# Two transformer layers on one core: norm arithmetic moved to GpSimd, reciprocals spread by DMA, and the two ends of the schedule reordered

## The chip, the core and the metric

The kernel runs on one core of one Trainium2 chip. A core has five engines that run side by side: TensorE (PE, the matmuls; PEld are its weight loads), VectorE (DVE), ScalarE (ACT), GpSimd (POOL) and SyncE (SP, which here issues DMAs). They share an on-chip memory of 128 partitions; matmuls write to a second one, PSUM, of eight banks per partition, here 512 fp32 columns each. The metric is the device time of one execution in microseconds, the median of several runs. Lower is better.

## The reference

Two layers of attention and feed-forward on 2048 rows of 512 features, both layers with the same weights. Attention has 32 heads of only 16 features each; the feed-forward part has 1792 hidden features.

```python
def _layernorm(x, axis=-1, eps=1e-5):
    m = jnp.mean(x, axis=axis, keepdims=True)
    v = jnp.var(x, axis=axis, keepdims=True)
    return (x - m) / jnp.sqrt(v + eps)

def _A_ref(x, wqkv, wo):                     # S = 2048, D = 512, H = 32, Dh = 16
    q, k, v = ...                            # x @ wqkv, split into 32 heads
    scores = jnp.einsum("bhqd,bhkd->bhqk", q, k) * (Dh ** -0.5)
    p = _softmax(scores, axis=-1)
    o = jnp.einsum("bhqk,bhkd->bhqd", p, v)
    return o.reshape(B, S, D) @ wo           # (after a transpose of heads and rows)

def _B_ref(x, w1, w2):                       # w1: 512 x 1792, w2: 1792 x 512
    return jnp.maximum(x @ w1, 0) @ w2

x = A_x
x = x + _A_ref(_layernorm(x), A_wqkv, A_wo)
x = x + _B_ref(_layernorm(x), B_w1, B_w2)
x = x + _A_ref(_layernorm(x), A_wqkv, A_wo)
x = x + _B_ref(_layernorm(x), B_w1, B_w2)
```

Per layer there are 32 heads x 2048 x 2048 scores, and each needs an exponential.

## The kernel before

The kernel is a Python program that writes the instruction stream of each engine. While it does so it keeps estimates of where PE and VectorE stand (`now_pe`, `now_dve`) and decides with them what comes next. The estimates are of use only for the order: the order is fixed when the kernel is built.

**The unit of work.** A score block is 128 keys x 512 queries of one head (256 queries in the last part of layer two). A *segment* is one chunk of queries and one set of heads; it has up to 64 blocks (16 key blocks x 4 heads that run side by side in PE). In each *slot* PE writes the scores of three blocks into three PSUM banks, and ScalarE takes the exponential of all three in one instruction. In some slots VectorE takes the third block instead: it builds the exponential by integer arithmetic on the bits. Two such blocks make a *pair*, and a pair goes through a chain of steps.

```python
ex = nc.scalar.activation(                   # L1323: 3 blocks, or 2 when VectorE takes one
    out=eb[:, 0 : place[m]], in_=b[:, 0 : place[m]], func=ACTF.Exp,
    scale=1.0 / (LOG2E * UNIT),
)
...
first = nc.vector.tensor_scalar(             # L1008: VectorE's block, out of PSUM
    out=lin[which][:, half * QS : (half + 1) * QS], in0=src, scalar1=EXP_BIAS,
    scalar2=0.0, op0=ALU.add, op1=ALU.max,
)
...
steps = (                                    # chain(): the rest, on both blocks at once
    (342, lambda: bits(0x7F, 0x3F80)),                                           # step
    (609, lambda: nc.vector.tensor_mul(out=power, in0=mantissa, in1=mantissa)),  # cube
    (342, lambda: ...),                      # scaling by a constant, mostly left out
    (342, lambda: bits(0x7F80, 0)),                                              # step
    (609, lambda: nc.vector.tensor_mul(                                          # cube
        out=power.bitcast(BF16), in0=power, in1=line.bitcast(BF16))),
)
```

A pair is begun when the schedule's conditions allow it: among others at most five pairs may be open, in the first layer the last value block must have been made (one pair may be open before), and the estimate of VectorE's queue must be short enough.

```python
elif (not pairs or pair_no[0] + 1 - pairs[0]["n"] < NP) and (
    (mine['l'] or ("v", 0, 15) in made or not pairs and ("k", 0, 0, 1) in made) and ...):
    queued = sum(t["cost"] for t in dve_q if "chain" in t)
    ...
    if now_dve[0] + waiting < now_pe[0] + BACKLOG:
        ...
```

**Order on VectorE.** VectorE's tasks wait in a queue and are taken by rank; the steps of a pair come last, unless their segment is the current one and nearly over.

```python
def rank(t):
    if "chain" not in t:
        return 2
    sg = t["chain"]["sg"]
    return 1.5 if sg is segs[seg_at[0]] and sg["left"] <= HASTE else 3     # HASTE = 12
...
for sg, kb, g in taken:          # taken: only the blocks that go to VectorE
    sg["left"] -= 1
```

**The value matmuls.** The blocks are multiplied with the values and summed over keys into one PSUM bank, `ps_o` (L914). Right after its exponentials a slot makes sure that the values of its key blocks exist:

```python
for sg, kb, g in now:
    run_until(("v", sg["l"], kb))
```

**End of a segment.** An extra column of ones in the values gives the sums for the softmax. Where a segment covers only some of the keys, its sums are stored and added later (`sg["load"]`). At the end the sums are copied to `u`, a small DMA brings the row of sums into a packed form `c`, VectorE takes reciprocals, and another DMA brings them back into `u`. Then they must be spread over the 32 partitions of each head: either by a GpSimd-issued DMA, or, where it must be quick, by a VectorE shuffle.

```python
quick = sg["load"] is not None or ended[l, j] == NT
def recip():
    nc.vector.reciprocal(out=c, in_=c)
    nc.sync.dma_start(out=sums, in_=c)
    if not quick:
        nc.gpsimd.dma_start(out=r[:, 0:width], in_=...)    # L863, sums spread to 32 partitions
    ...
def spread():
    nc.vector.stream_shuffle(out=r[:, 0:width], in_=u[:, 0:width], mask=[lane] * 32)   # L873
def spread_mul():
    if quick:
        spread()
    mul(0, width)                                                                      # L849
```

**The norm.** For each chunk of rows VectorE makes statistics and aggregates them, then the inverse root is taken: a seed from the bits of the number, and three Newton steps, in the middle of the run on GpSimd (`ln_newton`), in the first and the last norm on VectorE.

```python
def ln_stats(tag, tt, i):
    nc.vector.bn_stats(out=st[:], in_=x_t[tt][:])
    nc.vector.bn_aggr(out=mv[ln_n(tag)][:, i, :], in_=st[:])

def ln_rstd(tag, part):
    if part == 0:
        nc.vector.tensor_scalar(out=a[:], in0=mv[n][:, :, 1], scalar1=EPS, ...)         # L485
        nc.vector.tensor_scalar(out=t1[:], ..., op0=ALU.logical_shift_right)            # L488
        nc.vector.tensor_scalar(out=y[:], ..., scalar2=float(RSQRT_SEED), ...)          # L492
        return
    ...                          # one Newton step, 3 operations on VectorE

def ln_newton(tag):
    for _ in range(3):           # 4 operations each, on GpSimd
        ...
```

**The start.** Warming matmuls, the first norm, a transpose of its rows by PE with copies alternating between VectorE and ScalarE, then the first keys, queries and two value groups, and only then the loop of slots.

**The end.** After the last slot: the last segment's sums, the output projection, the last norm, and the feed-forward part of the last 256 rows, with its weights `w1buf` loaded four ahead.

Of the kernel before, what the change touches and what calls it, by code (L numbers as in the profile page):

```python
# [19 lines left out]
EPS = 1e-5  # L20
RSQRT_SEED = 0x5F3759DF
# [3 lines left out]
def kernel(  # L25
# [55 lines left out]
    RSTD_LAG = 5000.0  # L81
# [22 lines left out]
    masks = sb([P, 4], FP32, "masks")  # L104
# [51 lines left out]
    stats = [sb([P, nc.vector.BN_STATS_DIM], FP32, f"stats{n}") for n in range(2)]  # L156
# [23 lines left out]
    nc.gpsimd.memset(warm[:], 0.0)  # L180
    nc.vector.memset(ebuf[0][:, 0:QS], 0.0)
# [166 lines left out]
    def rank(t):  # L348
        if "chain" not in t:
            return 2  # L350
        sg = t["chain"]["sg"]
        return 1.5 if sg is segs[seg_at[0]] and sg["left"] <= HASTE else 3
# [120 lines left out]
    def ln_stats(tag, tt, i):  # L473
        if tag not in ln_seq:
            ln_seq.append(tag)
        st = stats[i % 2]
        nc.vector.bn_stats(out=st[:], in_=x_t[tt][:])  # L477
        nc.vector.bn_aggr(out=mv[ln_n(tag)][:, i, :], in_=st[:])

    def ln_rstd(tag, part):  # L480

        n = ln_n(tag)
        a, y, t1 = va_[n], ya_[n], ta_[n]
        if part == 0:
            nc.vector.tensor_scalar(  # L485
                out=a[:], in0=mv[n][:, :, 1], scalar1=EPS, scalar2=None, op0=ALU.add
            )
            nc.vector.tensor_scalar(  # L488
                out=t1[:].bitcast(I32), in0=a[:].bitcast(I32), scalar1=1, scalar2=None,
                op0=ALU.logical_shift_right,  # L490
            )
            nc.vector.tensor_scalar(  # L492
                out=y[:].bitcast(I32), in0=t1[:].bitcast(I32), scalar1=-1.0,
                scalar2=float(RSQRT_SEED), op0=ALU.mult, op1=ALU.add,
            )
            return
        nc.vector.scalar_tensor_tensor(
            out=t1[:], in0=y[:], scalar=-0.5, in1=y[:], op0=ALU.mult, op1=ALU.mult
        )
        nc.vector.tensor_mul(out=t1[:], in0=t1[:], in1=a[:])  # L500
        nc.vector.scalar_tensor_tensor(
            out=y[:], in0=t1[:], scalar=1.5, in1=y[:], op0=ALU.add, op1=ALU.mult
        )

    def ln_newton(tag):

        n = ln_n(tag)
        a, y, t1 = va_[n], ya_[n], ta_[n]
        for _ in range(3):
            nc.gpsimd.tensor_mul(out=t1, in0=y, in1=y)  # L510
            nc.gpsimd.tensor_mul(out=t1, in0=t1, in1=a)
            nc.gpsimd.tensor_scalar(
# [968 lines left out]
```

## Time and profile before

| | before |
|---|---|
| device time, median of 3 runs | 1611.67 us (1610.54 to 1612.03) |
| profiled execution, span | 1606.2 us |
| ScalarE busy | 1558.0 us (97%) |
| VectorE busy | 1505.7 us (94%) |
| PE busy (pipelined, modelled ends) | 1446.1 us (90%) |
| GpSimd busy | 92.9 us (6%) |
| exponentials on ScalarE (L1323) | 1366 instructions |
| blocks on VectorE (L1008) | 680, in 340 pairs |
| norm statistics / aggregations on VectorE | 64 / 64 |
| shuffles of reciprocals on VectorE (L873) | 28 |
| broadcasts of reciprocals by DMA (L863) | 52 |

How to read the lines of a profile: L1323 is line 1323 of the kernel; then come the engine and the operation, output<-input with partitions x elements and type, and the count. After the first bar stand busy time in us and the mean of one in ns, after the second the idle time of that engine just ahead of these instructions and what ended it ("<-PE ps_s L1314": a matmul into `ps_s`). A line of the time line begins with start and length in us. A busy share is an average over the run; a wait counts only on the engine that sets the end.

### The profile page before, as it was taken

To read this page: it belongs to the slowest core of one execution; us is meant where nothing else is said; L and a number is where in the kernel's file an instruction comes from. 1 tells how busy PE (TensorE), PEld (TensorE's weight loads), DVE (VectorE), ACT (ScalarE), POOL (GpSimd) and SP (SyncE) were. 2 spreads that over 40 slices of the span, in tenths; PEclk is the share of its full clock that TensorE was granted. 3 is DMA by queue.
4 is the path that set the end of the run, shared out by engine and by line. 5 is a ranking of instruction groups with operands and counts; after the bars stand their busy time and mean duration, and the time that the engine had idled before them with its cause. 6 is when DMAs were issued, how large, how long until landed. Compare 5 with 4: busy or idle time off the path is not lost. (4 is left out here: it accounts for less than half of the span.)

```text
span 1606.2 us, 45384 instructions
## 1 busy us (share of the span) xinstructions
PE 1446.1 (90%) x19833; PEld 541.9 (34%) x19833; DVE 1505.7 (94%) x3012; ACT 1558.0 (97%) x1385; POOL 92.9 (6%) x279
## 2 busy tenths in 40 slices
PE   7988888999999988999889998889989999998997
PEld 3322222322332332232223333223334444544454
DVE  7779999999999999999899999899999999999994
ACT  6999999999999999999999999999999999999994
POOL 2000001000010010100100000001001010010100
PEclk9999999999999999999999999999999999999999
DMA  5000000210001100120001000000210211212031
GB/s 164 2 2 2 2 2 9 47 29 10 9 17 40 28 16 2 27 50 10 15 2 27 21 2 1 2 4 9 54 24 17 42 30 29 59 28 54 14 62 47
DMA packets 113928, 40.61 MB, mean 25 GB/s; under 512 B 103328, under 2 KB 111264, under 8 KB 113728
## 3 DMA queue, kind: packets, MB, share of 16 engines
q1 hardware_dynamic: 101696, 26.21, 7.2%
q0 software_dynamic: 10688, 10.18, 3.6%
q8 instruction: 155, 2.54, 0.7%
q10 hardware_dynamic: 1344, 1.31, 0.2%
q14 instruction: 45, 0.37, 0.1%
HBM read 24.38 MB, written 2.10 MB: 16 GB/s over the span
## 5 line engine op out<-in xcount | busy, mean ns | idle before, releaser
L1323 ACT ACTIVATE e<-ps_s 128x1536 bf16<-128x1536 f32 (+1 forms) x1366 | 1548.1, 1364 | 12.4 <-PE ps_s L1314 7.7
L1314 PE MATMUL ps_s<-q,ktp 32*128 32x512 bf16 (+1 forms) x6192 | 613.6, 341 | 112.2 <-ACT e L1323 97.5
L914 PE MATMUL ps_o<-e,vaug 128*32 128x512 bf16 (+1 forms) x4262 | 501.0, 346 | 16.6 <-DVE u L836 6.8
L1008 DVE TENSOR_SCALAR lin<-ps_s 128x512 int16<-128x512 f32 x680 | 462.3, 684 | 32.9 <-PE ps_s L1314 27.4
L1314 PEld LDWEIGHTS <-ktp 32*128 32x128 bf16 x6192 | 199.9, 91 | 561.5 <-issue 417.5
L914 PEld LDWEIGHTS <-vaug 128*32 128x32 bf16 x6032 | 171.5, 94 | 305.0 <-issue 286.2
L1049 DVE TENSOR_SCALAR step<-lin 128x1024 int16<-128x1024 int16 x680 | 266.2, 417 | 1.1 <-PE ps_o L914 0.4
L1060 DVE TENSOR_TENSOR cube<-step 128x1024 f16<-128x1024 bf16 x340 | 230.2, 680 | 0.9
L1064 DVE TENSOR_TENSOR cube<-cube,lin 128x1024 bf16<-128x1024 f16 x340 | 229.5, 677 | 0.0
L914 PE MATMUL ps_o<-step,vaug 128*32 128x512 bf16 (+1 forms) x858 | 154.3, 341 | 0.0
L442 PE MATMUL ps_f<-xnT,w 128*32 128x512 bf16 (+1 forms) x2016 | 147.4, 345 | 5.7 <-DVE ht L695 3.7
L442 PE MATMUL ps_f<-w,ht 128*32 128x512 bf16 x1624 | 147.1, 381 | 1.6 <-DVE q L637 0.6
L914 PE MATMUL ps_o<-cube,vthird 128*32 128x512 bf16 (+1 forms) x804 | 140.0, 339 | 0.0
L914 PE MATMUL ps_o<-lin,vaug 128*32 128x512 bf16 (+1 forms) x858 | 118.9, 341 | 4.6 <-DVE u L836 3.7
L442 PE MATMUL ps_f<-xnT,wqkv 128*32 128x512 bf16 (+1 forms) x1312 | 106.7, 363 | 3.6 <-DVE vaug L623 1.8
L863 POOL DMA_DIRECT2D r<-u x52 | 36.9, 710 | 1170.2 <-DVE step L1049 383.3
L442 PE MATMUL ps_f<-wo,ot 128*32 128x512 bf16 x960 | 87.1, 381 | 1.5 <-DVE x L661 0.7
L695 DVE TENSOR_SCALAR ht<-ps_f 128x512 bf16<-128x512 f32 x105 | 71.8, 684 | 3.6 <-PE ps_f L442 3.0
L442 PEld LDWEIGHTS <-w 128*32 128x32 bf16 x2016 | 58.4, 96 | 36.0 <-issue 19.2
L637 DVE TENSOR_TENSOR q<-ps_f,masks 128x1024 bf16<-128x1024 f32 (+1 forms) x51 | 53.5, 1049 | 3.5 <-PE ps_s L1314 2.6
L442 PEld LDWEIGHTS <-ht 128*32 128x32 bf16 x1624 | 47.0, 96 | 27.3 <-issue 12.1
L849 DVE SCALAR_TENSOR_TENSOR ot<-u,masks,r 128x512 bf16<-128x512 f32 (+2 forms) x82 | 51.0, 624 | 1.1
(86 smaller groups left out, 653.4 us busy)
## 6 DMA issues: line engine op xcount, KB each, us to landing
w<-in_B_w_dram SPq DMA_DIRECT2D x140, 128.0 KB
r<-u POOLq DMA_DIRECT2D x25, 256.0 KB, 7.3
r<-u POOLq DMA_DIRECT2D x27, 128.0 KB, 4.9
out_dram<-x SPq DMA_DIRECT2D x16, 128.0 KB
x<-in_A_x_dram SPq DMA_DIRECT2D x14, 128.0 KB
w<-in_B_w_dram SPq DMA_DIRECT2D x1, 1792.0 KB
wqkv<-in_A_wqkv_dram ACTq DMA_DIRECT2D x2, 512.0 KB
c<-u SPq DMA_DIRECT2D x48, 8.0 KB
```

The lines of the kernel that those rows point to most:

```text
L442: nc.tensor.matmul(out[cols], lhsT[:, cols], rhs, start=i % k == 0, stop=i % k == k - 1, tile_position=(0, 32 * g), skip_group_check=True,)
L637: return nc.vector.tensor_mul(out=qbuf[n % 2][:, :, 0:w], in0=b.rearrange("p (e q) -> p e q", e=1).to_broadcast((P, 2, w)), in1=qmask.rear ...
L695: nc.vector.tensor_scalar(out=out, in0=sums, scalar1=0.0, scalar2=None, op0=ALU.max)
L849: nc.vector.scalar_tensor_tensor(out=ot[t][:, at_column + a : at_column + a + w], in0=u[:, a : a + w], scalar=mask[e], in1=r[:, a : a + w] ...
L863: nc.gpsimd.dma_start(out=r[:, 0:width], in_=bass.AP(tensor=sums.tensor, offset=sums.offset, ap=[list(sums.ap[0]), [0, 32], [1, width]],),)
L914: nc.tensor.matmul(ps_o[32 * g : 32 * g + 32, 0 : sg["w"]], values[:, 4 * sg["T"] + g, 2 * e : 2 * e + 32], rhs, start=g not in sg["begun" ...
L1008: first = nc.vector.tensor_scalar(out=lin[which][:, half * QS : (half + 1) * QS], in0=src, scalar1=EXP_BIAS, scalar2=0.0, op0=ALU.add, op1 ...
L1049: nc.vector.tensor_scalar(out=stair, in0=line, scalar1=keep, scalar2=put, op0=ALU.bitwise_and, op1=ALU.bitwise_or,)
L1060: (609, lambda: nc.vector.tensor_mul(out=power, in0=mantissa, in1=mantissa)),
L1064: (609, lambda: nc.vector.tensor_mul(out=power.bitcast(BF16), in0=power, in1=line.bitcast(BF16))),
L1314: nc.tensor.matmul(b[:, a : a + sg["w"]], kt[32 * g : 32 * g + 32, kc : kc + P], qbuf[sg["n"] % 2][32 * g : 32 * g + 32, sg["e"], 0 : sg[" ...
L1323: ex = nc.scalar.activation(out=eb[:, 0 : place[m]], in_=b[:, 0 : place[m]], func=ACTF.Exp, scale=1.0 / (LOG2E * UNIT),)
```

## The change

The norm in the middle of the run leaves VectorE but for its statistics: nine small GpSimd operations aggregate, add epsilon and take the inverse root with a power. The first and the last norm stay on VectorE with a seed in one operation and two refining steps instead of three. Stored sums that are longer than four key blocks (those of the first layer's first chunk) get their reciprocals spread by DMA, and where the shuffle is kept, it and the multiply are two tasks. Values are made when the value matmuls want them and no longer at each slot. The counter `left` counts every block, and the haste rule holds for any segment. At the start the copies, the first value groups and the order of keys and queries change; at the end the last sums are used right out of PSUM, and the last chunk's weights are loaded a stage ahead into buffers that are free by then.

```diff
+    nc.gpsimd.memset(masks[:, 4:5], -0.5)
-    RSTD_LAG = 5000.0
+    RSTD_LAG = 4000.0
@@ rank
-        return 1.5 if sg is segs[seg_at[0]] and sg["left"] <= HASTE else 3
+        return 1.5 if sg["left"] <= HASTE else 3
@@ norm, middle of the run
-        nc.vector.bn_stats(out=st[:], in_=x_t[tt][:])
-        nc.vector.bn_aggr(out=mv[ln_n(tag)][:, i, :], in_=st[:])
+        nc.vector.bn_stats(out=stats[ln_n(tag)][:, i, :], in_=x_t[tt][:])
+            pool = nc.gpsimd
+            pool.tensor_tensor(out=t1, in0=st[:, :, 1], in1=st[:, :, 4], op=ALU.subtract)
+            pool.tensor_mul(out=t1, in0=t1, in1=t1)
+            pool.tensor_scalar(out=t1, in0=t1, scalar1=0.25, scalar2=EPS, op0=ALU.mult, op1=ALU.add)
+            pool.tensor_add(out=a, in0=st[:, :, 2], in1=st[:, :, 5])
+            pool.tensor_scalar(out=a, in0=a, scalar1=1.0 / D, scalar2=None, op0=ALU.mult)
+            pool.tensor_add(out=a, in0=a, in1=t1)
+            pool.tensor_add(out=mean, in0=st[:, :, 1], in1=st[:, :, 4])
+            pool.tensor_scalar(out=mean, in0=mean, scalar1=0.5, scalar2=None, op0=ALU.mult)
+            pool.tensor_tensor(out=ya_[n][:, 0:rows], in0=a, in1=masks[:, 4:5].to_broadcast((P, rows)), op=ALU.pow)
@@ first and last norm: aggregations, then 9 VectorE operations instead of 12
+        ln_seed(tag, rows, GAIN)
+        nc.vector.tensor_mul(out=t1, in0=y, in1=y)
+        nc.vector.tensor_mul(out=t1, in0=t1, in1=a)
+        stt(out=t1, in0=t1, scalar=-10.0 / 3.0, in1=t1, op0=ALU.add, op1=ALU.mult)
+        stt(out=y, in0=t1, scalar=5.0, in1=y, op0=ALU.add, op1=ALU.mult)
+        ...
@@ end of a segment
-        musts.append((77 + 1.045 * width, now_pe[0] + PE_TO_DVE, copy))
+        if last:
+            sums_wait[0] -= 1
+        else:
+            musts.append((77 + 1.045 * width, now_pe[0] + PE_TO_DVE, copy))
-        quick = sg["load"] is not None or ended[l, j] == NT
+        quick = ended[l, j] == NT or sg["load"] is not None and sg["busy"]
...
+            if quick:
+                task(200 + 1.05 * width, spread, [("spread", n)], [ready])
+                ready = ("spread", n)
+            task(105 + 1.1 * width, lambda: mul(0, width), ots + [("m", n)], [ready] + war)
@@ which blocks the value matmuls may take
+        def value_made(kb):
+            key = ("v", sg["l"], kb)
+            return key in made and at([key], "pe") <= t
...
@@ the loop of slots
-        for sg, kb, g in taken:
+        for sg, kb, g in now:
             sg["left"] -= 1
-        for sg, kb, g in now:
-            run_until(("v", sg["l"], kb))
@@ start
-        copy = nc.scalar.copy if i % 2 else nc.vector.tensor_copy
+        copy = nc.vector.tensor_copy if i > 1 else nc.scalar.copy
...
-    for kb in range(2):
-        b = plain(v_mms(kb))
-        uses(nc.scalar.copy(out=v_out(0, kb), in_=v_in(b)), in_bank[0])
-        mark(("v", 0, kb))
-    work.extend(v_group(0, kb) for kb in range(2, TPC))
+    b = plain(v_mms(0))
+    uses(nc.vector.tensor_copy(out=v_out(0, 0), in_=v_in(b)), in_bank[0])
+    mark(("v", 0, 0))
+    work.extend(v_group(0, kb) for kb in range(1, TPC))
@@ estimates at the loop's start
-    now_pe[0] = 12000.0
-    now_dve[0] = 13400.0
-    exp_end = {-1: 13600.0, 0: 13600.0}
+    now_pe[0] = 13160.0
+    now_dve[0] = 14500.0
+    exp_end = {-1: 12600.0, 0: 13600.0}
@@ end: the last chunk's weights, loaded when the chunk two before it begins its rest
+                home = (
+                    w1buf[((l * NQS + LAST) * NF + ft) % NW1] if ft < NW1
+                    else (kt01 + kt2)[(ft - NW1) // 2][:, ft % 2, :].rearrange(
+                        "p (c f) -> p c f", c=NDC)
+                )
...
-                    b, w1buf[n % NW1][:, c, :], xnT[NQS - 1][:, c, at_column : at_column + width],
+                    b, w1_last[ft][:, c, :], xnT[NQS - 1][:, c, at_column : at_column + width],
-            load_w1(n + NW1)
```

## The prediction

> **What bounds the kernel now.** I read the page's engine shares first, then the groups with shapes kept apart, then ScalarE alone along the time line, and last the two ends of the run. The engine shares of the kernel before:
>
> ```profile
> span 1606.2 us, 45384 instructions
> PE 1446.1 (90%) x19833; PEld 541.9 (34%) x19833; DVE 1505.7 (94%) x3012; ACT 1558.0 (97%) x1385; POOL 92.9 (6%) x279
> ```
>
> Three engines are nearly full, and ScalarE (ACT) is the fullest. Its work is the exponential of the attention scores. The groups by shape (count, busy us, mean ns of one) show how that work is split with VectorE (DVE):
>
> ```profile
> L1323 ACT ACTIVATE e<-ps_s 128x1536 bf16<-128x1536 f32 x685 | 1026.9, 1574 | 8.2 <-PE ps_s L1314 4.2 <-PE ps_o L914 3.6
> L1323 ACT ACTIVATE e<-ps_s 128x1024 bf16<-128x1024 f32 x680 | 733.1, 1153 | 4.2 <-PE ps_s L1314 3.5 <-PE ps_o L914 0.4
> ...
> L1008 DVE TENSOR_SCALAR lin<-ps_s 128x512 int16<-128x512 f32 x680 | 462.3, 684 | 32.9 <-PE ps_s L1314 27.4
> ...
> L1049 DVE TENSOR_SCALAR step<-lin 128x1024 int16<-128x1024 int16 x680 | 266.2, 417 | 1.1 <-PE ps_o L914 0.4
> L1060 DVE TENSOR_TENSOR cube<-step 128x1024 f16<-128x1024 bf16 x340 | 230.2, 680 | 0.9
> L1064 DVE TENSOR_TENSOR cube<-cube,lin 128x1024 bf16<-128x1024 f16 x340 | 229.5, 677 | 0.0
> ```
>
> Every slot has three score blocks. In 680 of the 1366 slots one of them goes to VectorE, which builds the exponential from integer and multiply steps, two blocks (a pair) at a time. One block off ScalarE saves 1574 - 1153 = 421 ns; one pair saves 0.842 us. One pair costs VectorE (462.3 + 266.2 + 230.2 + 229.5, and 10.2 for a fifth step that few pairs need) / 340 = 3.52 us. So this is a balance: a microsecond freed on VectorE is worth a microsecond only after it has been turned into pairs, at a rate worked out below.
>
> ScalarE's own time line between the first and the last exponential has few gaps (start, length, group, then the idle time before it and what ended it):
>
> ```profile
> 16.74 136.69 ACT L1323 ACTIVATE e<-ps_s 128x1536 bf16<-128x1536 f32 x112 [0.51 <-PE ps_s L1314]
> 153.83 1.02 ACT L1323 ACTIVATE e<-ps_s 128x1024 bf16<-128x1024 f32 x1 [0.40 <-PE ps_o L914]
> 156.53 1.45 ACT L1323 ACTIVATE e<-ps_s 128x1536 bf16<-128x1536 f32 x1 [1.67 <-PE ps_o L914]
> 158.79 1.02 ACT L1323 ACTIVATE e<-ps_s 128x1024 bf16<-128x1024 f32 x1 [0.81 <-PE ps_s L1314]
> 160.30 1.45 ACT L1323 ACTIVATE e<-ps_s 128x1536 bf16<-128x1536 f32 x1 [0.49 <-PE ps_s L1314]
> 162.67 1.02 ACT L1323 ACTIVATE e<-ps_s 128x1024 bf16<-128x1024 f32 x1 [0.92 <-PE ps_s L1314]
> ```
>
> So the run is: 16.7 us before ScalarE starts, 1560 us in which it idles only 12.4 us (1548.1 busy), and some 29.5 us after its last exponential ends near 1576.7. The change can win at the front, at the end, in those 12.4 us, or by fewer blocks on ScalarE. Nothing else is on the path.
>
> [...] ScalarE is 97% busy, 99.2% inside its stage (1548.1 of 1560), and I don't take PE's 90% as a bound. [...] a 128x4 operation takes 162 to 170 ns here[...]. [...] GpSimd's tiny operations take 193 ns at least and up to 677 in the groups on the root's tile. [...] after the stall at 155 us matmuls of 512 columns take 0.61 us instead of 0.39, and the stage's granted clock is 0.86. [...]
>
> **The change part by part.**
>
> 1. *Norm on VectorE, middle of the run.* 16 of the 18 norms lie in the stage (the first and the last do not). Each loses three tiny VectorE operations (add epsilon, shift, seed). They start 0.20 us apart at 20.49, 20.69 and 20.89: 16 x 0.6 = 9.6 us. Of the 64 aggregations (182 ns) 58 go to GpSimd. In the time line a statistic with its aggregation repeats every 0.80 us (4.25, 5.05, 5.84), and a statistic alone is 0.66 us and a gap of 0.04: so 0.10 to 0.18 each, and 58 x 0.12 = 7 us. GpSimd then does 9 tiny operations instead of 12, at about 0.28 us each 2.5 us plus an unknown power: it has 94% of its time free, and the schedule waits 4 us instead of 5 for it.
>
> 2. *Stored sums' reciprocals by DMA.* Only the first chunk of the first layer has segments with loaded sums longer than four key blocks: 8 of them, the eighth still quick because it ends the chunk. 7 shuffles of 727 ns go: 5.1 us. In their place come 7 broadcasts from GpSimd's queue, 7.3 us to land, which others already use; the buffer of three sums covers that. Splitting the shuffle from the multiply also means that one task no longer holds VectorE for 0.72 + 0.75 us in a row.
>
>    Parts 1 and 2 free 9.6 + 7 + 5.1 = 21.7 us of VectorE. Turned into N pairs over a stage that gets 0.842 N shorter: 21.7 = N x (3.52 + 0.842), N = 5.0, and the time falls by **4.2 us**. I expect about 345 pairs instead of 340.
>
> 3. *Haste, values on demand, split tasks.* The counter of blocks left in a segment now counts all blocks and not only VectorE's, so the rule that pushes a pair's last steps ahead near the end of a segment becomes real. Before, a long segment started at 64 and lost only those few that VectorE took, and so almost never came down to 12. The cluster of gaps at 153.4 to 164.2 is 0.40 + 1.67 + 0.81 + 0.49 + 0.92 + 0.49 = 4.8 us. There a segment's end waited for VectorE (a shuffle, a multiply, then late chain steps), PE stood still, its clock fell, and it took 10 us to recover. I count this cluster as won, and the other 7.6 us as unchanged, since a new schedule will have stalls of its own: **-4.5 us**.
>
> 4. *Start.* Three tiny operations fewer: the seed is one operation instead of two, and one improved step and one usual one replace three: 3 x 0.2 less what the aggregations cost apart, about 0.4 us. The first two copies of the transposed rows go to ScalarE, which idles until 10.48; before, VectorE could copy only after its last scaling at 10.5. With both the keys' first matmul moves from 12.00 to about 11.4; its weights were let through at 11.46, so not much below. From there: 1.92 us to the query's masking, 1.23 for that, 0.2 to the scores, 0.43 from scores to exponential. Before, the scores stood behind two value groups and the next query's (16.31 instead of 15.3). First exponential at 11.4 + 3.8 = 15.2 instead of 16.74: **-1.5 us**.
>
> 5. *End.* The copy of the last sums goes: 0.42 us and a gap, 0.45. Three tiny operations of the last norm: 0.6. All weights of the last chunk are loaded a stage ahead; the feed-forward steps are 0.87 us apart, and one of them waits for its weights, 1597.60 to 1599.00, so 0.5. Sum **-1.6 us**.
>
> ```profile
> 1598.99 0.33 PEld L1377 LDWEIGHTS <-w 128*128 128x128 bf16 x4 [0.86 <-DMA w<-in_B_w_dram]
> ```
>
> This line is that wait; the other steps keep their pace, so early weights win only here.
>
> Sum: -4.2 - 4.5 - 1.5 - 1.6 = -11.8 us; 1611.7 - 11.8 = 1599.9.
>
> **The rivals.**
>
> *Freed VectorE time stays idle.* Pairs are admitted by a list of conditions of the schedule: no more than five open, and in the first layer none but one before the last value block is made. VectorE is busy only 65.7 of the 93 us from 17 to 110 already, so room alone makes no pairs. Then part 1 and 2 give nothing: -7.6 us, 1604. For it: those 27 idle us. Against it: from 200 us on VectorE is over 93% busy in every 100 us, where its room is what counts.
>
> *New stalls.* Value groups made only when they are wanted may come late; then the probability buffers fill and PE is forced. Or the promoted chain steps push back norms and output scalings, and the groups behind them starve at a chunk's end. Each cluster like that at 155 us costs 5 us. Two more of them than I count, and the result is about 1609. For it: the schedule is reshuffled as a whole, and PE has few spare slots. Against it: the conditions at the front are looser, and values are still made in the order of the queue.
>
> *More than the balance.* If the values come freely, the last one, which admits pairs in the first layer, comes earlier than the 115 us or so of now. Of the 34 idle us of VectorE before 200 us, half used would be 17 / 4.36 = 4 more pairs, 3.3 us more: with all gaps closed as well, about 1589.
>
> *GpSimd becomes a wait.* A power as slow as ten tiny operations would be 3 us more per norm, 16 norms. It would show only where a norm gates the next work; PE has other groups queued. At most 2 to 3 us.
>
> **Range and chances.** Ends and tiny operations, 5 to 8 us, are read off directly; the stalls may give -9 or cost +3. The time is 1600, the range 1591 to 1608. Faster by over 2% needs under 1579.4, 20 us beyond the sum and more than all gaps and both ends' savings together: 0.03. Slower by over 2% needs 1643.9, eight new clusters: 0.01. Within 2%: 0.96.
>
> **What would show it.** Right: first exponential at 15.2; about 345 pairs (690 of the 512-wide first steps on VectorE); ScalarE's stage with 8 us of gaps, and none of a microsecond near 155; VectorE's tiny operations gone from the stage and 21 shuffles in all; the end 28 us long with no wait for weights. Wrong: pairs unchanged at 340 with VectorE's share lower; gaps over 12 us, above all at chunk ends or with PE waiting for values; GpSimd's root holding up the scalings of rows. A first exponential still after 16 us would mean that the weights, not the norm, set the start.

## The result and the profile after

| | before | after |
|---|---|---|
| device time, median | 1611.11 us (1605.39 to 1612.03) | 1597.27 us (1595.39 to 1599.99, 4 runs) |
| ratio, 95% interval | | 0.9923 [0.9895, 0.995] |
| profiled execution, span | 1606.2 us | 1593.3 us |
| first exponential starts at | 16.74 us | 14.52 us |
| first to last exponential (the stage) | 1559.97 us | 1551.94 us |
| ScalarE busy / idle in the stage | 1548.1 / 11.9 us | 1544.6 / 7.4 us |
| VectorE busy / idle in the stage | 1480.7 / 79.3 us | 1468.9 / 83.1 us |
| last exponential to the end | 29.49 us | 26.84 us |
| blocks on VectorE | 680, in 340 pairs | 684, in 342 pairs |
| shuffles on VectorE / broadcasts by DMA | 28 / 52 | 21 / 59 |

The median of before is that of four runs. The time falls by 13.8 us, 0.8%; these are few runs, and in the experiments below, with 11 to 51 runs of the kernel before beside them, its median lies at 1607.97 to 1608.67 us and the fall at about 11. The engine shares on the page of the kernel after:

```profile
span 1593.3 us, 45167 instructions
...
PE 1437.3 (90%) x19793; PEld 539.0 (34%) x19793; DVE 1490.0 (94%) x2899; ACT 1553.2 (97%) x1383; POOL 98.4 (6%) x240
```

The bound is the same. VectorE has 113 instructions fewer and is busy 15.7 us less over the run, but ScalarE sets the time. Its groups, with shapes kept apart (count, then busy us and mean ns of one):

```profile
L1365 ACT ACTIVATE e<-ps_s 128x1536 bf16<-128x1536 f32 x681 | 1024.1, 1576 | 8.2 <-PE ps_s L1356 7.6 <-PE ps_o L944 0.5
L1365 ACT ACTIVATE e<-ps_s 128x1024 bf16<-128x1024 f32 x684 | 739.3, 1157 | 1.2 <-PE ps_s L1356 0.9
L1051 DVE TENSOR_SCALAR lin<-ps_s 128x512 int16<-128x512 f32 x684 | 465.5, 685 | 24.1 <-PE ps_s L1356 17.2 <-issue 0.3
...
L1092 DVE TENSOR_SCALAR step<-lin 128x1024 int16<-128x1024 int16 x684 | 268.8, 419 | 0.6
L1107 DVE TENSOR_TENSOR cube<-cube,lin 128x1024 bf16<-128x1024 f16 x342 | 232.3, 680 | 0.0
L1103 DVE TENSOR_TENSOR cube<-step 128x1024 f16<-128x1024 bf16 x342 | 231.8, 681 | 0.6
...
L496 POOL TENSOR_TENSOR ya<-va,masks 128x4 f32<-128x4 f32 x13 | 15.1, 1158 | 0.0
```

The durations are those of before within 0.5%; the counts moved by two pairs. The last line is the power on GpSimd: 1.16 us each. ScalarE's own time line in the stage (start, length, group, then the idle time before it and what ended it):

```profile
14.52 1.45 ACT L1365 ACTIVATE e<-ps_s 128x1536 bf16<-128x1536 f32 x1 [1.99 <-PE ps_s L1356]
...
128.93 448.09 ACT L1365 ACTIVATE e<-ps_s 128x1536 bf16<-128x1536 f32 x404 [0.18 <-PE ps_s L1356]
577.24 1.02 ACT L1365 ACTIVATE e<-ps_s 128x1024 bf16<-128x1024 f32 x1 [0.21 <-PE ps_s L1356]
578.74 194.18 ACT L1365 ACTIVATE e<-ps_s 128x1536 bf16<-128x1536 f32 x173 [0.48 <-PE ps_s L1356]
773.10 384.16 ACT L1365 ACTIVATE e<-ps_s 128x1536 bf16<-128x1536 f32 x339 [0.18 <-PE ps_s L1356]
1157.44 222.95 ACT L1365 ACTIVATE e<-ps_s 128x1536 bf16<-128x1536 f32 x198 [0.17 <-PE ps_s L1356]
1384.60 1.45 ACT L1365 ACTIVATE e<-ps_s 128x1536 bf16<-128x1536 f32 x1 [4.21 <-PE ps_s L1356]
1386.76 179.70 ACT L1365 ACTIVATE e<-ps_s 128x1024 bf16<-128x1024 f32 x160 [0.71 <-PE ps_s L1356]
```

The cluster at 155 us is gone: from 128.93 on, 404 exponentials run without a listed gap. In its place stands one new hole, 4.21 + 0.71 us at 1384. So 4.9 of the 7.4 idle us that are left belong to one spot.

In a sum over the two profiled executions: start -2.2, end -2.65, two more pairs at 0.842 us -1.7, idle time of ScalarE -4.5, and -1.8 of ScalarE's busy time that the pairs don't explain. Part of this last term is restarts: a three-block exponential that starts after a gap is recorded with 1.45 us, inside a stretch the next one adds 1.34 us (12.20 us for nine of them from 16.14 on: 1.45 + 8 x 1.34), so each gap costs about 0.1 us beyond itself, and there are 11 gaps fewer.

The two executions differ in one more thing: the clock granted to PE was 0.992 on average in the first and 0.996 in the second. The second pair of profiles below has 0.992 and 0.993. There the sum is 9.4 us instead of 12.9: start -2.15, stage -6.12, end -1.13, and ScalarE's idle time in the stage falls by 3.2 us, from 13.97 to 10.74.

### The profile page after: what moved, and what is told of

Read it like the earlier page. It is cut to its first block, busy times and chain, and to the rows that moved or that the text cites. A ratio compares the mean times of both kernels' runs of the same rounds, so it can differ in the third digit from the quotient of the medians.

```text
span 1593.3 us, 45167 instructions
## 1 busy us (share of the span) xinstructions
PE 1437.3 (90%) x19793; PEld 539.0 (34%) x19793; DVE 1490.0 (94%) x2899; ACT 1553.2 (97%) x1383; POOL 98.4 (6%) x240
## 4 chain that ended last, share of the span: by engine, by line
ACT 72%; PE 14%; DVE 11%; issue 2%; SPq 1%; DMA 0%; POOL 0%; ACTq 0%; DVEq 0%
ACT e L1365 72%; PE ps_s L1356 5%; PE ps_f L445 4%; PE ps_o L944 4%; DVE lin L1051 3%; DVE cube L1103 1%; DVE step L1092 1%; DVE cube L1107 1%; PE ps_s L1417 1%; DVE q L643 1%; DVE ht L701 1%; SPq L766 1%; DVE stats L479 0%; DVE u L858 0%; DVE x L727 0%
## 5 line engine op out<-in xcount | busy, mean ns | idle before, releaser
L1365 ACT ACTIVATE e<-ps_s 128x1536 bf16<-128x1536 f32 (+1 forms) x1366 | 1544.6, 1366 | 9.4 <-PE ps_s L1356 8.5
L1356 PE MATMUL ps_s<-q,ktp 32*128 32x512 bf16 (+1 forms) x6121 | 604.6, 340 | 106.2 <-ACT e L1365 96.3
L944 PE MATMUL ps_o<-e,vaug 128*32 128x512 bf16 (+1 forms) x4256 | 496.3, 345 | 12.4 <-DVE u L858 5.4
L1356 PEld LDWEIGHTS <-ktp 32*128 32x128 bf16 x6121 | 196.3, 91 | 552.2 <-issue 418.0
L445 PE MATMUL ps_f<-xnT,w 128*32 128x512 bf16 (+1 forms) x2016 | 151.0, 347 | 6.1 <-DVE ht L701 2.9
L944 PE MATMUL ps_o<-cube,vthird 128*32 128x512 bf16 (+1 forms) x812 | 148.9, 338 | 0.5 <-DVE cube L1107 0.5
L888 POOL DMA_DIRECT2D r<-u x59 | 43.7, 740 | 1176.8 <-DVE lin L1051 383.2
L445 PEld LDWEIGHTS <-w 128*32 128x32 bf16 x2016 | 60.0, 97 | 37.3 <-issue 21.7
L643 DVE TENSOR_TENSOR q<-ps_f,masks 128x1024 bf16<-128x1024 f32 (+1 forms) x51 | 53.6, 1051 | 12.4 <-PE ps_f L445 7.6
L944 PEld LDWEIGHTS <-vthird 128*32 128x32 bf16 x812 | 44.5, 95 | 30.6 <-issue 27.1
```

Source lines behind the costliest of these rows:

```text
L445: nc.tensor.matmul(out[cols], lhsT[:, cols], rhs, start=i % k == 0, stop=i % k == k - 1, tile_position=(0, 32 * g), skip_group_check=True,)
L643: return nc.vector.tensor_mul(out=qbuf[n % 2][:, :, 0:w], in0=b.rearrange("p (e q) -> p e q", e=1).to_broadcast((P, 2, w)), in1=qmask.rear ...
L888: nc.gpsimd.dma_start(out=r[:, 0:width], in_=bass.AP(tensor=sums.tensor, offset=sums.offset, ap=[list(sums.ap[0]), [0, 32], [1, width]],),)
L944: nc.tensor.matmul(ps_o[32 * g : 32 * g + 32, 0 : sg["w"]], values[:, 4 * sg["T"] + g, 2 * e : 2 * e + 32], rhs, start=g not in sg["begun" ...
L1356: nc.tensor.matmul(b[:, a : a + sg["w"]], kt[32 * g : 32 * g + 32, kc : kc + P], qbuf[sg["n"] % 2][32 * g : 32 * g + 32, sg["e"], 0 : sg[" ...
L1365: ex = nc.scalar.activation(out=eb[:, 0 : place[m]], in_=b[:, 0 : place[m]], func=ACTF.Exp, scale=1.0 / (LOG2E * UNIT),)
```

## The experiments

Stage and gaps are read from the profiled execution; gaps are the sum of the idle times in ScalarE's time line between the first and the last exponential (11.2 us before, 7.0 us after by this count; the table above also has the idle times too short to be listed). Ratios are against the kernel before, run on the same chip in between (medians 1607.97 to 1608.67 us); the runs were made on four chips, so where two kernels ran on different ones, the ratios compare them better than the microseconds do. The last column is the mean clock granted to PE in the profiled execution. Gaps go with it: two executions of one kernel differ by 2.3 us (before: 11.2 and 13.5) and 3.1 us (after: 7.0 at 0.996 and 10.1 at 0.993).

| run | median, us | ratio [95%] | stage | gaps | blocks on VectorE | clock |
|---|---|---|---|---|---|---|
| a0_after | 1597.57 | 0.9933 [0.9915, 0.9952] | 1556.05 | 10.1 | 684 | 0.993 |
| e1_spread_loads | 1595.10 | 0.9914 [0.9895, 0.9933] | 1550.83 | 5.2 | 684 | 0.993 |
| e2_loads_at_end | 1593.77 | 0.9907 [0.9888, 0.9926] | 1549.21 | 3.4 | 684 | 0.996 |
| e3_old_norm_same_order | 1607.76 | 0.9994 [0.9981, 1.0007] | 1567.04 | 18.2 | 684 | 0.987 |
| f4_old_norm_told | 1595.93 | 0.9923 [0.9911, 0.9935] | 1551.71 | 4.2 | 680 | 0.997 |
| f1_no_haste | 1593.39 | 0.9914 [0.9896, 0.9932] | 1547.60 | 3.0 | 686 | 0.998 |
| f2_old_quick | 1598.74 | 0.9938 [0.9924, 0.9952] | 1554.90 | 8.2 | 684 | 0.993 |
| f3_forced_values | 1596.67 | 0.9927 [0.9914, 0.994] | 1553.48 | 9.2 | 688 | 0.994 |
| b0_before | 1609.65 | 1.0009 [0.9999, 1.002] | 1562.17 | 13.5 | 680 | 0.992 |
| f5_ends_only | 1608.87 | 1.0008 [0.9994, 1.0022] | 1561.82 | 11.9 | 678 | 0.995 |
| g_h_p4 | 1615.46 | 1.0041 [1.0027, 1.0055] | 1571.89 | 29.5 | 700 | 0.985 |
| h_work_only | 1593.23 | 0.9914 [0.9898, 0.993] | 1549.46 | 5.3 | 688 | 0.999 |

### The kernel after once more, and the hole at 1384

The first run repeats the kernel after unchanged, as the measure for the others.

> The changed kernel once more, as the reference point for the runs beside it: 1597 us, within 3 us, and again one gap of some 4 us on ScalarE near 1384 us of the span.

It came out at 1597.57 us (1595.36 to 1600.12), the same as the first measurement, with the hole at 1384 again (4.73 + 0.71 us). So the hole belongs to the order. The time line of the kernel after around it (SPq is the DMA queue that SyncE issues):

```profile
1371.75 6.69 SPq L766 DMA_DIRECT2D ktp<-in_B_w_dram  x7
...
1372.76 0.41 DVE L858 COPY u<-ps_o 128x256 f32<-128x256 f32 x1
...
1378.54 0.56 SPq L863 DMA_DIRECT2D c<-u  x1
...
1380.58 0.20 DVE L885 RECIPROCAL c<-c 128x8 f32<-128x8 f32 x1 [3.75 <-DMA c<-u]
...
1382.33 0.40 PE L944 MATMUL ps_o<-step,vaug 128*32 128x256 bf16 x2 [3.17 <-DVE step L1092]
...
1384.60 1.45 ACT L1365 ACTIVATE e<-ps_s 128x1536 bf16<-128x1536 f32 x1 [4.21 <-PE ps_s L1356]
```

The sums of a finished segment are copied to `u` by 1373.17. The small DMA that packs them (`c<-u`) is issued only at 1378.54: the last chunk's ten early weight loads stand in front of it in SyncE's queue, issued in a row from 1369.87 on, the last seven of them in the 6.69 us of the first line. VectorE, whose next operation at 1376.83 is the reciprocal of these sums, waits 3.75 us for them; then PE waits 3.17 us for VectorE's steps, and ScalarE 4.21 us for PE. Two kernels test this. The first issues the loads one at a time, after each feed-forward group; the order of all computing stays the same:

```diff
-                    nc.sync.dma_start(out=home, in_=B_w1[:, ft * P : (ft + 1) * P]...)
+                    to_load.append((home, ft))
@@ feed-forward group
+            load_one()            # issues one of them
```

> The ten early loads of the last chunk's weights are issued one after each feed-forward group instead of all at once; the order on the compute engines is the same. Theory (the ten issues block SyncE for 6.7 us and with it the transfer of the sums that VectorE waits for): the gaps of 4.21 and 0.71 us near 1384 us vanish, the stage is 5 to 6 us shorter, the end unchanged: about 1592 us. Rival (a stall at a segment's end like others, the loads only happen to stand there): the gap stays within 1 us of its size, and the time is 1597 us.

```profile
1161.55 404.14 ACT L1372 ACTIVATE e<-ps_s 128x1536 bf16<-128x1536 f32 x359 [0.17 <-PE ps_s L1363]
```

```profile
1377.31 0.56 SPq L870 DMA_DIRECT2D c<-u  x1
```

The first of these two lines is ScalarE's, the second SyncE's. The copy of the sums to `u` ends at 1377.29 in e1, and the small DMA is issued 0.02 us later, where in the kernel after it was 5.4 us.

The second loads the weights at the end, four ahead, as the kernel before did:

```diff
-        if n < len(chunks) * NF - NF + NW1:
+        if n < len(chunks) * NF:
-        if (l, j) == (1, LAST - 2):          # the early loads
+        if False:
-                    b, w1_last[ft][:, c, :], ...
+                    b, w1buf[((l * NQS + j) * NF + ft) % NW1][:, c, :], ...
+            load_w1((l * NQS + j) * NF + ft + NW1)
```

> The last chunk's weights are loaded four ahead at the end, as before the change; all else as changed, the same order on the compute engines. Theory of the early loads: the gap near 1384 us vanishes as well (-5 us), and the end, 26.8 us with early weights, becomes 0.5 us longer for the one wait for weights: about 1592.5 us, so that the early loads as they stand cost more than they bring. Rival (the feed-forward part at the end, 1.9 us shorter than before, owes all of it to the early weights): the end grows to 28.7 us, 1594 us.

In both the hole is gone: with spread loads, as the line of e1's time line shows, 359 exponentials run through 1384 without a listed gap. Against the repeat of the kernel after, e1 is 2.5 us faster and e2 3.8 us; about 5 were expected. In the profiles e1's stage is 5.2 us shorter than that of the repeat at the same clock, but its end took 28.6 us: seven matmuls of the output projection took 3.19 us there (from 1566.32) and 1.67 in e2. Of the other profiles with early weights seven have an end of 26.5 to 27.4 us, those of f1 and f2 one of 28.2; with late ones it is 26.91 in e2, against 26.84 in both profiles of the kernel after: the early weights bring next to nothing, 0.07 us. The part of the change that was to save half a microsecond at the end costs 3 to 5 us in the stage. All four runs of e2 (1593.36 to 1593.96) are faster than every run of both kernels.

### The norm

The norm's old operations (aggregation, epsilon and seed on VectorE, three Newton steps on GpSimd) are put back into the kernel after, once without telling the schedule's estimates, so that the order stays the same:

```diff
-            pool.tensor_tensor(out=ya_[n][:, 0:rows], in0=a, in1=masks[:, 4:5]..., op=ALU.pow)   # and 8 more
+            nc.vector.tensor_scalar(out=a, in0=mv[n][:, 0:rows, 1], scalar1=EPS, ...)
+            nc.vector.tensor_scalar(out=t1..., op0=ALU.logical_shift_right)
+            nc.vector.tensor_scalar(out=y..., scalar2=float(RSQRT_SEED), ...)
+            for _ in range(3): ...                               # 4 GpSimd operations
+            nc.vector.bn_aggr(out=mv[ln_n(tag)][:, i, :], ...)   # with each statistic
```

> The norm in the middle of the run as before the change (58 aggregations and 48 tiny operations back on VectorE, twelve Newton operations on GpSimd), but with the schedule not told, so that every engine keeps the order of the changed kernel. VectorE gets 16 to 19 us more work. Theory (VectorE and ScalarE are both bound from 200 us on, work added without fewer pairs delays the score banks): +5 to +10 us on the run beside it. Rival (VectorE's 83 idle us take it up): under +2 us.

and once on top of e1 with the estimates set back too:

```diff
-            task(720, lambda: ln_stats...
+            task(830, lambda: ln_stats...
-            task(0, rstd, ...        RSTD_LAG = 4000.0
+            task(500, rstd, ...      RSTD_LAG = 5000.0
```

> On the kernel with the loads spread (1595 us): the norm of the middle as before the change, and this time the schedule knows its costs, so it orders anew and takes 680 blocks on VectorE instead of 684. Theory (the balance of the prediction: a microsecond of VectorE is worth 0.193 us once the order has adapted): 16.6 x 0.193 = +3.2 us, 1598. Rival (what the run with the fixed order showed: every microsecond on VectorE falls on the path, order or not): +10 us, 1605.

Untold, the old norm costs 10.2 us (1607.76 against 1597.57) for 11.2 us more of VectorE's time (1501.5 against 1490.3; 16 to 19 were expected). Part of this is a lower clock: its median is 0.9905 over the 14 runs, 0.995 in the five of the kernel after beside them. Runs of both at 0.992 take 1605.10 to 1606.53 and 1599.99 to 1600.12 us, some 6 us apart. One place in e3's time line shows such a fall of the clock:

```profile
763.10 1.38 DVE L535 TENSOR_SCALAR xn<-x,mv,ya 128x512 bf16<-128x512 bf16 x4 [0.93 <-POOL ya L505]
...
763.57 0.61 PE L544 MATMUL ps_f<-ident,xn 128*128 128x128 bf16 x4 [0.95 <-DVE xn L535]
...
764.76 2.54 ACT L1374 ACTIVATE e<-ps_s 128x1024 bf16<-128x1024 f32 x2 [1.20 <-PE ps_s L1365]
```

VectorE waits 0.93 us for the root on GpSimd and PE 0.95 us for VectorE; PE's granted clock falls to 0.50 from about 763.6 to 773.8, and ScalarE is without scores for 1.20 us, and 2.2 us more in the next 10. In the kernel after VectorE waits 1.12 us for the root at the same place (758.20) and PE 0.61 us for VectorE; the clock stays at 1.00 from 757 to 775 and ScalarE has no listed gap. Told, the same work costs 0.8 us (1595.93 against 1595.10), or 1.4 by the ratios, whose intervals overlap: the schedule makes two pairs fewer, and its gaps are 4.2 us. The two kernels ran on different chips; at a clock of 0.995 and 0.996 the told one takes 1595.65 to 1596.26 us and e1, in two runs, 1594.16 and 1592.24, so that the 3.2 us of the balance are not excluded. That wrong estimates cost more than the norm's work itself is shown; how many times more is not.

### The rules of the schedule, and the shuffles

Three more single parts were each undone on top of e1. First the haste rule with its counter:

```diff
-        return 1.5 if sg["left"] <= HASTE else 3
+        return 1.5 if sg is segs[seg_at[0]] and sg["left"] <= HASTE else 3
-        for sg, kb, g in now:
+        for sg, kb, g in taken:
```

> On the kernel with the loads spread (1595 us): the rank rule and the counter of blocks left as before the change. 686 blocks on VectorE instead of 684. Theory (the haste rule closed the gaps at segments' ends): gaps of 1 us and more come back on ScalarE, +4.5 us, 1599.5. Rival (the gaps went with the shuffles, or with the values on demand): within 1 us of 1595, and the stretch from 140 to 170 us stays free of gaps.

Then the shuffles and the joint task:

```diff
-        quick = ended[l, j] == NT or sg["load"] is not None and sg["busy"]
+        quick = sg["load"] is not None or ended[l, j] == NT
-            if quick: task(200 + 1.05 * width, spread, ...)
-            task(105 + 1.1 * width, lambda: mul(0, width), ...)
+            task(cost, both, ...)                   # shuffle and multiply in one
```

> On the kernel with the loads spread (1595 us): the seven stored sums of the first layer spread by VectorE's shuffle again, and shuffle and multiply in one task. 684 blocks, as many as with the DMA. Theory (5.1 us of VectorE at 0.193): +1 us, 1596. Rival (the long task of 1.5 us made the stall near 155 us): gaps of 1 us and more return between 130 and 200 us, +5 us, 1600.

Then the values made at every slot:

```diff
+        for sg, kb, g in now:
+            run_until(("v", sg["l"], kb))
```

> On the kernel with the loads spread (1595 us): values are made sure of at every slot again, as before the change. 688 blocks on VectorE instead of 684, which alone would be 4 x 0.42 = 1.7 us less on ScalarE. Theory (values on demand keep PE free of forced work): new gaps in the first 130 us, +2 us, 1597. Rival (nothing waits for the values either way): -1.7 us, 1593.4.

Without the haste rule the kernel is not slower (1593.39 us against 1595.10, 686 blocks, gaps 3.0), and no gap lies between 130 and 200 us. The theory that haste removed the cluster fell. The shuffles cost 3.6 us (1598.74), with new gaps of 2.01 and 1.01 us at 1179 to 1184 and none between 130 and 200; forced values 1.6 us (1596.67) though two pairs more are made, with 3.0 us of gaps before 130 us instead of 0.9. The intervals of all these ratios overlap with e1's, so none of these costs is clear of the spread. No single part of the middle carries the gain, and the cluster at 155 us comes back in none of the three.

### Is the cluster the order's, or chance?

> The kernel before once more, for a second profile of it: about 1608 us. Theory of the prediction (the gaps between 153 and 164 us belong to its order: a segment's end waits for VectorE): again a gap of 1.5 us or more near 155 us and 4 us or more of gaps between 130 and 200 us. Rival (a half-rate stretch of PE's clock that fell there in one execution): under 1 us of gaps in that stretch, and gaps elsewhere.

The kernel before once more; ScalarE's time line:

```profile
153.75 1.02 ACT L1323 ACTIVATE e<-ps_s 128x1024 bf16<-128x1024 f32 x1 [0.39 <-PE ps_o L914]
156.22 1.45 ACT L1323 ACTIVATE e<-ps_s 128x1536 bf16<-128x1536 f32 x1 [1.45 <-PE ps_o L914]
158.49 1.02 ACT L1323 ACTIVATE e<-ps_s 128x1024 bf16<-128x1024 f32 x1 [0.81 <-PE ps_s L1314]
160.00 1.45 ACT L1323 ACTIVATE e<-ps_s 128x1536 bf16<-128x1536 f32 x1 [0.49 <-PE ps_s L1314]
162.37 1.02 ACT L1323 ACTIVATE e<-ps_s 128x1024 bf16<-128x1024 f32 x1 [0.92 <-PE ps_s L1314]
```

The same gaps at the same places, 4.8 us in all. It is the order's. Then a kernel with only the two ends of the change (start, sums out of PSUM, shorter last norm, weights ahead but spread); norm, shuffles, values, rank and counter are as before; only the condition that a block's values must exist before it is multiplied stays as after:

```diff
 # e1, with f4 (old norm, told), f1 (old rank and counter), f2 (old shuffles) and f3 (forced values) all undone
```

> Of the change only the start and the end (with the weights' loads spread out); norm of the middle, shuffles, values, rank and counter as before. 678 blocks on VectorE, two fewer than before: +0.8 us. Theory (the two ends are worth what the profiles show, 2.2 and 2.65 us, and the stage stays as before): 1608 - 4.9 + 0.8 = 1604. Rival (a new start reshuffles the whole order, and that alone moves the stage): a stage more than 3 us off that of before, gaps near 155 us gone or moved; 1600 or 1608 us.

```profile
14.88 1.45 ACT L1384 ACTIVATE e<-ps_s 128x1536 bf16<-128x1536 f32 x1 [2.40 <-PE ps_s L1375]
...
19.74 1.45 ACT L1384 ACTIVATE e<-ps_s 128x1536 bf16<-128x1536 f32 x1 [1.58 <-PE ps_s L1375]
...
153.43 115.17 ACT L1384 ACTIVATE e<-ps_s 128x1536 bf16<-128x1536 f32 x104 [0.27 <-PE ps_s L1375]
...
277.59 381.07 ACT L1384 ACTIVATE e<-ps_s 128x1536 bf16<-128x1536 f32 x341 [1.08 <-PE ps_o L963]
...
1183.07 11.40 ACT L1384 ACTIVATE e<-ps_s 128x1024 bf16<-128x1024 f32 x10 [1.10 <-PE ps_s L1375]
```

This kernel is not faster than the kernel before (1608.87, 1603.36 to 1617.57 over 22 runs), though its first exponential is 1.8 us earlier. The new start moves the cluster away: 0.27 us is all there is between 130 and 200 us. But the idle time only went elsewhere: 11.9 us of gaps in the stage, among others at 18, 270 to 277, 766 and 1183 us. The stage is as long as that of before (1561.82 against 1559.97 and 1562.17 us), and the theory's 4 us did not come. Closing one visible cluster by a new order was no gain here, with VectorE as full as it was (busy 1479.9 of the stage's 1561.8 us).

### More pairs at the front

VectorE idles most between 20 and 110 us (59 of 90 us busy after the change), because the first layer admits one pair only until the last value block is made. On e2 up to four pairs were allowed there:

```diff
-("v", 0, 15) in made or not pairs and ("k", 0, 0, 1) in made
+("v", 0, 15) in made or len(pairs) < 4 and ("k", 0, 0, 1) in made
```

> The changed kernel with the last weights loaded at the end as before, and with up to four pairs instead of one allowed before the last value block of the first layer is made: 700 blocks on VectorE instead of 684. Theory (VectorE's 27 idle us before 110 us can be turned into pairs): 16 x 0.42 = -6.7 us on 1593.8, 1587 us. Rival (the early pairs hold up the copies of keys and values): gaps of 3 us and more before 130 us, 1593 us or more.

The theory fell. Eight pairs more than e2's 684 blocks take ScalarE's busy time down, but 18.9 us of gaps open before 130 us (2.09 us at 71, 2.08 at 88, 7.75 at 106), and the time is 21.7 us above e2. All engines' time line in the largest gap:

```profile
106.09 0.38 PE L535 MATMUL ps_f<-ident,xn 128*128 128x128 bf16 x4 [1.38 <-DVE q L643]
...
106.51 0.42 DVE L576 COPY xnT<-ps_f 128x512 bf16<-128x512 bf16 x1 [0.47 <-PE ps_f L535]
106.99 0.38 PE L535 MATMUL ps_f<-ident,xn 128*128 128x128 bf16 x4 [0.52 <-DVE xnT L576]
...
112.03 0.69 DVE L593 CAST ktp<-ps_f 128x512 bf16<-128x512 f32 x1 [2.00 <-PE ps_f L445]
...
113.43 1.45 ACT L1365 ACTIVATE e<-ps_s 128x1536 bf16<-128x1536 f32 x1 [7.75 <-PE ps_s L1356]
```

The keys that the next scores need are not made yet. PE and VectorE take turns over four transposes and four copies, then come the keys' matmuls and their copy (`ktp`), from 106.1 to 112.7, and nothing else is there to fill PE. e2 has no such gap. So the preparation of the first layer came late where more pairs were let in before it. That VectorE's idle time at the front is what keeps it prompt fits this, but two or three pairs were not tried.

### VectorE's work alone

Last, the work is taken off VectorE (norm and shuffles as in the change) and the rules are as before (rank, counter, forced values):

```diff
 # e1, with f1 (old rank and counter) and f3 (forced values) undone
```

> On the kernel with the loads spread (1595 us): the rank rule, the counter and the values at every slot as before the change, while the norm stays off VectorE and the stored sums stay on the DMA. The four middle parts undone one by one cost +0.8, -1.7, +3.6 and +1.6 us, 4 us together; undone all at once (the run with the ends only) they cost 14. This run undoes the two rules and keeps the two that take work off VectorE. Theory (VectorE's work decides: with the work gone the rules don't matter): 1593 to 1597 us, a stage of 1552 us or less. Rival (the rules are what lets the stage use the freed time; work alone gives little): 1601 us or more, gaps of 9 us or more on ScalarE.

It takes 1593.23 us, as the theory said. This kernel and f5 have the same old rules and ends and differ in norm and shuffles, on VectorE or off it (with the estimates that go with them, and shuffle and multiply as one task or two): 15.6 us, 15.1 by the ratios. Some of it goes with the clock, whose median is 0.993 in the runs of f5 and 0.9985 here: at 0.994 and 0.995 f5 takes 1605.83 to 1608.65 us and this kernel 1596.06 and 1596.99, so about 10 us are there at an equal clock. Both stages as one window each (length, then busy us and count of PE, PEld, DVE, ACT, POOL, then granted clock, DMA share and GB/s), first f5, then this kernel:

```profile
14.88:1576.70 1561.82, 1410.34 (x19625) 523.68 (x19626) 1479.91 (x2937) 1549.16 (x1366) 91.55 (x244) 0.99 0.11 23
```

```profile
14.51:1563.97 1549.46, 1404.88 (x19685) 520.59 (x19685) 1473.90 (x2848) 1543.48 (x1366) 97.36 (x203) 1.00 0.12 25
```

VectorE is busy 6.0 us less with five pairs more (678 to 688 blocks). Five pairs are 5 x 3.52 = 17.6 us of work, so 23.6 us of other work left it. ScalarE is busy 5.7 us less, and its idle time in the stage falls from 12.7 to 6.0 us. That is more than two executions of one kernel differ by, and it is not only the clock: in windows of 5 us from 25 to 1555 us, those with a full clock (0.99 or more) hold 7.3 us of ScalarE's idle time in f5 and 2.3 here. For the kernel before the same count gives 4.9 and 6.8 us in its two profiles, for the kernel after 1.6 and 1.6. What PE waited for from 14 to 1570 us fits this (us in total, times, the longest), first in f5, then here:

```profile
PE ps_o L963 <- DVE u L874: 11.2, 26, 0.8
PE ps_s L1375 <- DVE lin L1070: 6.5, 12, 1.2
```

```profile
PE ps_o L951 <- DVE u L865: 8.2, 22, 0.8
...
PE ps_s L1363 <- DVE lin L1058: 2.7, 7, 0.9
```

PE waits less for VectorE to clear the banks of the sums (`u`) and of the scores (`lin`).

## Why the prediction was right, and where it was not

1. *Norm and shuffles* (21.7 us off VectorE, five pairs, -4.2 us). The direction of the work was right, its size only roughly: put back in the same order, the norm adds 11.2 us to VectorE's busy time where 16.6 were counted. The term of the pairs was too large for the kernel as it was changed: VectorE's busy time in the stage fell by 11.8 us with two pairs more (7.0 us), so 18.8 us went, and only two pairs, 1.7 us, were made of it. The rest is 8.0 us of a shorter stage and 3.8 us more idling. The comparison of f5 with the work alone gives five pairs, from 23.6 us. With the work off VectorE the new rules cost pairs: 688 blocks with the old rules, 684 with both new ones, 686 with only haste undone, 688 with only the values. So the first rival (freed time stays idle) was half right, for a cause that the prediction did not name.

2. *Haste and the cluster* (-4.5 us). The sum of the idle time fell by just that, 11.9 to 7.4 (13.97 to 10.74 in the second pair of profiles), but this agreement is luck: the step is the one that failed. The haste rule has no part in it (f1, and the work alone, do without); the new start moves the cluster by itself (f5), and then the same idle time stands elsewhere. What closed gaps here was room on VectorE: 12.7 us of idle time with its old work, 6.0 without, rules and ends alike. The prediction counted this room only as pairs; it buys about as much again as idle time of ScalarE. PE's score matmuls wait 2.7 us for VectorE instead of 6.5, which fits, though the gaps were not traced one by one. Undone one at a time, norm (told) and shuffles cost 0.8 and 3.6 us, together under the old rules 15.6. As far as the intervals go the effect is not a sum, but the rules differ too. Both undone under the new rules was not run, so how much the rules soften it stays open; so does why the new start spares the cluster at 155. In reading the lines of before, the prediction took the 0.86 of the window from 140 to 160 us for the stage's clock, which is 0.99 (0.50 was granted from 156 to 162 us), and its 12.4 us of idle time include 0.5 ahead of the first exponential.

3. *Start* (-1.5 us, measured -2.2). The mechanism was right, the keys' matmul was put too late: 11.4, measured 10.88, in the time line of the kernel after.

```profile
10.88 1.89 PE L1158 MATMUL ps_s<-xnT,wqkv 128*128 128x512 bf16 x8 [0.18 <-DVE xnT L1148]
...
12.81 1.23 DVE L643 TENSOR_TENSOR q<-ps_s,masks 128x1024 bf16<-128x1024 f32 x1 [0.88 <-PE ps_s L1158]
```

It waits for the transposed rows from VectorE, not for weights, so 11.46 was no limit. From there to the first exponential the chain takes 3.64 us; 3.8 was predicted. Over all profiles with this start the first exponential lies between 14.34 and 15.28.

4. *End* (-1.6 us, measured -2.65). In the profile of before that the prediction used, the feed-forward part ran at a granted clock of 0.90; in the repeat it was 1.00 and the end 27.97 us. Against that the change saves 1.13 us, which is what was worked out for the copy of the sums and the shorter norm (0.45 + 0.6). The 0.5 for early weights failed: 0.07. The other 1.5 us of the measured 2.65 go with the clock of one execution.

5. *What was not foreseen* is the hole at 1384, 4.9 us, from loads that were counted as free because they lay off the path. Without it the mechanisms would have given 1593.8 (e2). That the total came within 3 us of the prediction (1599.9, measured 1597.27) is in part luck: too few pairs and the hole on one side, fewer gaps of other kinds, a better start and a higher clock on the other.

GpSimd as a wait did not come about: the rival put 2 to 3 us on it at most, and VectorE waits once for the root, 1.1 us.

## What to carry to other kernels

When two engines are nearly full and one feeds the other's buffers, work taken off the second can buy more than the exchange rate says, because a late step of it can become a gap on the first, as at 1384 in the kernel after, where VectorE's wait of 3.75 us was followed by one of 3.17 on PE and 4.21 on ScalarE: here 23.6 us of it were worth about 10 us at an equal clock, where the rate gives 4.6. A schedule made from estimates must be told of any such change, for the untold version lost 10.2 us, clock included, and the told one 1 to 3. Read the clock of both executions before comparing their gaps. A transfer that is off the path was not free here: the small one behind it in the queue was issued 5.4 us late, with 4.9 us of gaps on ScalarE. Ask what stands behind it. A gap that disappears in a new order is not won until the sum of the gaps is smaller.

## What the hardware showed beyond this

PE's granted clock fell to 0.50 for some 12 us without a long stall before it. The same kernel in two executions, the repeat first and then the first profile of after, in two windows of 3 us (columns as above):

```profile
385.00:388.00 3.00, 1.87 (x22) 0.53 (x17) 3.00 (x7) 3.00 (x4) 1.55 (x3) 0.96 0.01 3
388.00:391.00 3.00, 2.93 (x21) 0.60 (x24) 2.21 (x7) 2.44 (x3) 0.00 (x0) 0.50 0.05 8
```

```profile
385.00:388.00 3.00, 1.92 (x22) 0.56 (x17) 3.00 (x7) 3.00 (x4) 1.60 (x3) 1.00 0.01 3
388.00:391.00 3.00, 2.82 (x32) 1.00 (x32) 3.00 (x8) 3.00 (x4) 0.00 (x0) 1.00 0.04 8
```

Until 388 both do the same with PE 62 to 64% busy from 385 on, and the longest idle stretch of PE from 383 on is 0.73 us in both; then one is granted 0.50 until about 400, PE manages 21 matmuls instead of 32 in 3 us, and ScalarE runs out of scores. This stretch alone is 3.4 us of gaps. What brings the fall about is not shown: before it PE was 36 to 38% idle in both executions, in small pieces, and the clock fell in only one. Over 51 runs of the kernel before, time and mean granted clock lie on a line (correlation -0.96): from 1603.83 us at 0.996 to 1616.71 at 0.986, about 1.1 us per 0.001. The median clock is 0.993 there and 0.995 after the change. At an equal 0.996 lines through these runs and the nine of the kernel after give 1604.3 and 1596.5, so some 8 of the 11 to 14 us are there at an equal clock. Kernels run side by side on one chip differ in their median clock (0.995 for the kernel after, 0.9905 for e3), so the order seems to have a part in it; that the rest of the gain follows from fewer stalls of PE is not shown.
